# Moving a general-case branch into the attention loop, building the bias on ScalarE, and starting the gated products at the last scores

## The chip, the cores and the metric

The kernel runs on one core of one Trainium2 chip. The metric is the device time of one execution in microseconds (us), lower being better; the runs shown are whole executions, and one further execution was taken with the hardware profiler. Engines are named as in the profile: PE is TensorE (PEld its weight loads), DVE is VectorE, ACT is ScalarE, POOL is GpSimd, SP is SyncE, which issues most of the DMAs. A queue name ends in q (DVEq is VectorE's sequencer).

## What is computed

Three stages follow each other: attention with a window of local keys plus a few global ones, a gated feed-forward layer with RMS normalisation, and a routed layer with eight experts. Cut to what matters here:

```python
def _attn_ref(q, k, v, n_global, n_local):          # q, k, v: 2 x 8 heads x 768 x 64
    scores = scale * np.matmul(q, k.transpose(0, 1, 3, 2))
    rel = pos[:, None] - pos[None, :]
    keep = is_global | ((rel >= 0) & (rel < n_local))
    dist = np.where(is_global & ~is_local, n_local, np.abs(rel))
    scores = np.where(keep, scores - slopes[:, None, None] * dist, -1e9)
    a = np.exp(scores - scores.max(-1, keepdims=True))
    return np.matmul(a / (a.sum(-1, keepdims=True) + 1e-9), v)

def _moe_ref(x, w_gate, w_val, w_out, rms_g):       # x: 1536 x 512, w_gate, w_val: 512 x 1536
    xn = x / np.sqrt(np.mean(x * x, -1, keepdims=True) + 1e-6) * rms_g
    g = xn @ w_gate
    return (g * sigmoid(g) * (xn @ w_val)) @ w_out
```

`n_global` is 8 and `n_local` is 96. They are inputs, so the kernel reads them at run time: if the window is narrow enough it takes a fast path (a block of 64 queries sees at most 192 keys), else a general one. The routed layer behind it is not touched by the change.

## The kernel before

**Attention.** The sixteen heads are taken in eight pairs (`pr`), each pair's 768 queries in three groups (`g`) of 256: 24 items. `attention` is a generator of 28 steps `t`, a software pipeline of five stages: step `t` computes the scores of item `t` (`qk`, line 240), divides item `t-1` by its denominators (`zadd` L267, `zrec` L271, `norm` L278), transposes item `t-2` on TensorE (`trans`, L286) and copies it out of PSUM (`evac`, L295 and L297), multiplies item `t-3` with V (`pv`, L313), and hands item `t-4` to the normalisation (`out`). Between these, VectorE adds bias to the scores and takes their minimum in one custom operation (`ttr`, L251), and ScalarE takes the exponentials (`exp`, L262). Every engine executes in the order in which the code issues; nothing reorders it. Steps 24 to 27, without new scores, are the drain.

**Bias.** `consts` (L59 to L77) makes `s.nl` and `s.ng` from the integers, then the flag of the fast path, which every engine loads into a register (L77). Behind it stands `tc.If(flag == 0)` around `general_attention` (L985 in the rows). Then `bias_tiles` builds `keep` and `miss` (L106 to L109) and, with four VectorE operations for each of four pairs of heads (L112), the bias tiles: the first pair's before step 0, the others after steps 0, 1 and 2.

**Normalisation.** `Rms.take` (L414 to L416) splits each output into `xh` and `xl` and squares it on ScalarE (`sq`, a tile for each pair). `add` (L422) sums squares on GpSimd after pairs 1 and 2 of each batch, leaving two tiles. `stats` (L444) sums them over partitions with matmuls against a 128 by 128 tile of ones, two times six for a batch, after step 17 for the first batch and after steps 26 and 27 for the second. `root` (L448 to L472) computes an inverse square root on VectorE and six diagonal tiles, three of them on ScalarE; `spread` (L478, L481) turns these into rows by matmuls and copies them out on ScalarE.

**Weights and gated products.** The 64-bit weights come in units. `unpack` takes a unit apart in five parts: an absolute value on ScalarE (L489), a comparison on VectorE (L491), two bit operations on VectorE (L496, L498), and a last one (L501) with a cast on ScalarE (L503) and a subtraction on GpSimd (L504). Four units are wanted for the first products. From step 13 on, one part follows each step (`next(unit)`). `gemm1` (L538) is a gated product, 24 matmuls over 512 or 256 columns; `gate1` (L549 to L556) evaluates the gate of the product before it. The first three products are issued behind steps 25, 26 and 27, the fourth behind the root; then the spreading, then the loop over `order`, whose first product is `(0, 1, 256, 512)`.

Of the kernel before, what the change touches and what calls it, by code (L numbers as in the profile page):

```python
# [43 lines left out]
def consts(s, ints):  # L44
# [23 lines left out]
    s.ng, s.nl = s.gl[:, 0:1], s.gl[:, 1:2]  # L68
    a = c.tile([128, 3], F32, name="fasta")
# [24 lines left out]
def bias_tiles(s):  # L94

    nc = s.nc
    s.kinds = [0, 64, 192, 384]
    N = 576  # L100
    s.bias = s.apool.tile([128, 4, N], F32, name="bias", bufs=1)
    rel, key = s.rel[:, 0:N], s.rel[:, N:2 * N]
    keep, miss, slopes = s.keep, s.miss, s.slopes
    nc.gpsimd.tensor_copy(slopes, s.rel[:, 2 * N:])
    spans = [(0, 64, 0), (64, 192, 4), (192, 384, 0), (384, 576, 4)]
# [12 lines left out]
def general_attention(s):  # L118

    nc, tc = s.nc, s.tc  # L120
    with tc.tile_pool(name="ga", bufs=1) as p, tc.tile_pool(name="gap", bufs=1, space=PSUM) as ps:
        slopes = p.tile([128, 8, 2], F32, name="gslopes")
        for j in range(16):
            nc.gpsimd.memset(slopes[:, j // 2, j % 2:j % 2 + 1], -(2.0 ** -(j % 8 + 1)))
        with tc.For_i(0, 8, 1) as pr:
            slope = p.tile([128, 2], F32, name="gslope")
            nc.vector.tensor_copy(slope, slopes[:, ds(pr, 1), :].rearrange("p a b -> p (a b)"))
            for hh in range(2):
                r = slice(64 * hh, 64 * hh + 64)
                q = p.tile([64, 768], F32, name="gq")  # L130
                nc.sync.dma_start(q.rearrange("p (a n) -> p a n", a=1),
                                  s.qx.rearrange("a p n -> p a n")[r, ds(pr, 1), :])
                k = p.tile([64, 928], F32, name="gk")
                nc.sync.dma_start(k.rearrange("p (a n) -> p a n", a=1),
                                  s.kx.rearrange("a p n -> p a n")[r, ds(pr, 1), :])
                v = p.tile([128, 11, 64], F32, name="gv")
                nc.sync.dma_start(v.rearrange("p (a b) d -> p a b d", a=1),
                                  s.vx.rearrange("a p h b d -> p a h b d")[:, ds(pr, 1), hh])
                xo = p.tile([64, 768], F32, name="gxo")
                rel0 = p.tile([128, 768], F32, name="grel0")  # L140
                nc.gpsimd.iota(rel0, pattern=[[-1, 768]], base=0, channel_multiplier=1,
                               allow_small_or_imprecise_dtypes=True)
                key0 = p.tile([128, 768], F32, name="gkey0")
                nc.gpsimd.iota(key0, pattern=[[1, 768]], base=0, channel_multiplier=0,
                               allow_small_or_imprecise_dtypes=True)
                with tc.For_i(0, 6, 1) as i:
                    qi = p.tile([64, 128], F32, name="gqi")
                    nc.vector.tensor_scalar(qi.rearrange("p (a c) -> p a c", a=1),
                                            q.rearrange("p (i c) -> p i c", c=128)[:, ds(i, 1), :],
                                            0.125, None, ALU.mult)  # L150
                    rel = p.tile([128, 768], F32, name="grel")
                    nc.vector.tensor_copy(rel, rel0)
                    key = p.tile([128, 768], F32, name="gkey")
                    nc.vector.tensor_copy(key, key0)
                    loc = p.tile([128, 768], F32, name="gloc")
                    dist, keep = distance(s, rel, key, loc)
                    sc = ps.tile([128, 6, 128], F32, name="gsc")
                    for j in range(6):
                        nc.tensor.matmul(sc[:, j, :], lhsT=qi, rhs=k[:, 160 * j:160 * j + 128],
                                         start=True, stop=True)  # L160
                    t = p.tile([128, 768], F32, name="gt")
                    nc.vector.scalar_tensor_tensor(
                        out=t, in0=dist, scalar=slope[:, hh:hh + 1], in1=sc.rearrange("p a b -> p (a b)"),
                        op0=ALU.mult, op1=ALU.add)
                    nc.vector.tensor_tensor(t, t, keep, ALU.mult)
                    nc.vector.tensor_scalar(keep, keep, 1.0, -NEG, ALU.subtract, ALU.mult)
                    nc.vector.tensor_tensor(t, t, keep, ALU.add)
                    m = p.tile([128, 1], F32, name="gm")
                    nc.vector.tensor_reduce(m, t, AX.X, ALU.max)
                    nc.vector.tensor_scalar(t, t, m, None, ALU.subtract)  # L170
                    z = p.tile([128, 1], F32, name="gz")
                    nc.scalar.activation(t, t, AF.Exp, accum_out=z)
                    nc.vector.tensor_scalar(z, z, 1e-9, None, ALU.add)
                    nc.vector.reciprocal(z, z)
                    nc.vector.tensor_scalar(t, t, z, None, ALU.mult)
                    pt = ps.tile([128, 6, 128], F32, name="gpt")
                    for j in range(6):
                        nc.tensor.transpose(pt[:, j, :], t[:, 128 * j:128 * j + 128], s.ident)
                    pts = loc.rearrange("p (a b) -> p a b", a=6)
                    nc.vector.tensor_copy(pts, pt)  # L180
                    po = ps.tile([64, 128], F32, name="gpo")
                    for j in range(6):
                        nc.tensor.matmul(po, lhsT=v[:, 2 * j, :], rhs=pts[:, j, :],
                                         start=j == 0, stop=j == 5)
                    nc.vector.tensor_copy(xo.rearrange("p (i c) -> p i c", c=128)[:, ds(i, 1), :],
                                          po.rearrange("p (a c) -> p a c", a=1))
                    nc.vector.tensor_scalar(rel0, rel0, 128.0, None, ALU.add)
# [754 lines left out]
def attn_moe_kernel(ctx, tc, qx, kx, vx, rel, ints, wgv, w_out, rms_g, w9, w9t, w1, w2, out):  # L942
# [96 lines left out]
    for t in att:  # L1039
# [5 lines left out]
        if t >= 13:  # L1045
            next(unit, None)
# [384 lines left out]
```

## Time and profile before

| | us |
|---|---|
| median of three runs | 554.47 (553.97 to 555.34) |
| the profiled execution | 554.08, span 552.3 |
| first minimum of the scores starts | 10.12 |
| last item's denominators (step 24) | 90.63 |
| first gated product starts | 99.14 |
| statistics of the second batch done | 118.10 |
| product `(0, 1, 256, 512)` starts | 123.28 |

The span is the time from the first to the last instruction in the profile. The rows name an instruction by its line, engine, operation and tiles; a float32 matmul of the code leaves two records, one for each pass. A number in square brackets is the idle time of the engine just before the row, with what ended it.

### The profile page before, as it was taken

How to read it: one execution, taken by the hardware profiler on the slowest of the kernel's cores; microseconds unless marked ns; L12 is line 12 of the kernel's file. 1: busy time of each engine (PE TensorE's matmuls, PEld its weight loads, DVE VectorE, ACT ScalarE, POOL GpSimd, SP SyncE). 2: the span in 40 equal slices, each digit the busy share in tenths (PEclk: the TensorE clock that was granted, in tenths of full speed). 3: DMA queues.
4: the chain of work that ended last, by engine and by line, in shares of the span. 5: the costliest groups of instructions: out<-in, count | busy, mean ns of one | idle time of the engine just before them, and what ended most of it. 6: DMA issues, size and time to landing. Idle time of an engine off the chain costs nothing. (4 is left out here: it accounts for less than half of the span.)

```text
span 552.3 us, 9096 instructions
## 1 busy us (share of the span) xinstructions
PE 524.2 (95%) x3132; PEld 425.8 (77%) x3132; DVE 404.8 (73%) x1026; ACT 277.5 (50%) x631; POOL 140.8 (25%) x140
## 2 busy tenths in 40 slices
PE   3899886999999999999999999999999999999994
PEld 2676665878888888888888888878789787888883
DVE  5899999567888688868884358456443599999971
ACT  2799896324332233333333255244231587988850
POOL 2446545001222212212220200000000512666001
PEclk9999998999999999999999999999999999999998
DMA  8653511112323323323313512116171599999300
GB/s 301 210 211 139 173 36 39 33 46 77 105 88 113 113 79 114 114 79 113 115 38 130 214 39 78 39 52 215 39 293 57 202 393 395 398 399 396 131 15 16
DMA packets 28997, 80.62 MB, mean 146 GB/s; under 512 B 3512, under 2 KB 3768, under 8 KB 28945
## 3 DMA queue, kind: packets, MB, share of 16 engines
q1 hardware_dynamic: 24400, 68.61, 35.0%
q0 software_dynamic: 2672, 8.22, 3.9%
q10 hardware_dynamic: 1872, 3.15, 1.6%
q8 instruction: 26, 0.43, 0.3%
q14 instruction: 27, 0.21, 0.1%
HBM read 72.28 MB, written 8.65 MB: 147 GB/s over the span
## 5 line engine op out<-in xcount | busy, mean ns | idle before, releaser
L538 PE MATMUL ps<-xh,wh 128*128 128x512 f32 (+1 forms) x304 | 115.4, 380 | 0.1
L538 PE MATMUL ps<-xh,wl 128*128 128x512 f32 (+1 forms) x304 | 115.0, 378 | 0.5 <-POOL wl L504 0.5
L538 PE MATMUL ps<-xl,wh 128*128 128x512 f32 (+1 forms) x304 | 114.9, 378 | 0.0
L854 DVE TENSOR_TENSOR ewl<-eraw,ewh 128x1024 fp32r<-128x1024 f32 x72 | 83.5, 1220 | 6.2 <-ACT ewh L845 5.9
L845 ACT CAST ewh<-eraw 128x1024 fp32r<-128x1024 f32 x72 | 71.3, 1055 | 6.2 <-DVE ewl L854 4.2
L538 PEld LDWEIGHTS ps<-xh,wl 128*128 128x128 f32 x304 | 57.2, 188 | 11.6 <-POOL wl L504 0.9
L491 DVE SCALAR_TENSOR_TENSOR wraw<-f64t,wraw 128x512 f32<-128x512 f32 x36 | 44.7, 1241 | 28.8 <-ACT f64t L489 28.8
L538 PEld LDWEIGHTS ps<-xh,wh 128*128 128x128 f32 x304 | 57.2, 188 | 11.0 <-issue 0.7
L538 PEld LDWEIGHTS ps<-xl,wh 128*128 128x128 f32 x304 | 57.2, 188 | 10.6
L604 PE MATMUL px<-woh,hh 128*128 128x512 f32 (+1 forms) x156 | 61.8, 396 | 0.0
L604 PE MATMUL px<-woh,hl 128*128 128x512 f32 (+1 forms) x156 | 58.7, 376 | 0.0
L604 PE MATMUL px<-wol,hh 128*128 128x512 f32 (+1 forms) x156 | 58.2, 373 | 0.0
L504 POOL TENSOR_TENSOR wl<-f64t,wh 128x512 fp32r<-128x512 f32 x24 | 31.0, 1293 | 101.3 <-ACT wh L503 55.7
L503 ACT CAST wh<-f64t 128x512 fp32r<-128x512 f32 x24 | 14.9, 622 | 71.4 <-DVE f64t L501 68.1
L262 ACT ACTIVATE es<-es,m 128x192 f32<-128x192 f32 (+1 forms) x96 | 41.4, 434 | 11.5 <-DVE m L251 10.3
L278 POOL TENSOR_SCALAR es<-es,z 128x192 f32<-128x192 f32 x46 | 36.0, 791 | 36.2 <-ACT pts L297 11.7
L286 PE MATMUL pt<-ident,es 128*128 128x128 f32 x176 | 30.5, 305 | 10.1 <-DVE pts L295 6.6
L286 PEld LDWEIGHTS pt<-ident,es 128*128 128x128 f32 x176 | 20.7, 152 | 21.6 <-DVE pts L295 10.0
L568 DVE TENSOR_TENSOR hl<-h,hh 128x256 fp32r<-128x256 f32 x72 | 25.4, 422 | 15.8 <-ACT hh L567 15.8
L604 PEld LDWEIGHTS px<-woh,hl 128*128 128x128 f32 x156 | 29.3, 188 | 5.8
L604 PEld LDWEIGHTS px<-woh,hh 128*128 128x128 f32 x156 | 29.4, 188 | 4.9
L604 PEld LDWEIGHTS px<-wol,hh 128*128 128x128 f32 x156 | 29.5, 189 | 4.0
(195 smaller groups left out, 979.7 us busy)
## 6 DMA issues: line engine op xcount, KB each, us to landing
eraw<-in_w_dram SPq DMA_DIRECT2D x64, 512.0 KB, 11.2
wraw<-in_wgv_dram SPq DMA_DIRECT2D x24, 512.0 KB, 3.8
wraw<-in_w_out_dram SPq DMA_DIRECT2D x12, 512.0 KB, 3.5
vp<-in_vx_dram SPq DMA_DIRECT2D x8, 704.0 KB, 4.0
eraw<-in_w_dram POOLq DMA_DIRECT2D x8, 512.0 KB, 13.6
kd<-in_kx_dram SPq DMA_DIRECT2D x7, 464.0 KB
xm<-x SPq DMA_DIRECT2D x12, 256.0 KB
out_dram<-x ACTq DMA_DIRECT2D x12, 256.0 KB, 2.8
```

Source lines behind the costliest of these rows:

```text
L262: nc.scalar.activation(e[:, r, x, e0:e0 + n], e[:, r, x, e0:e0 + n], AF.Exp, bias=m[:, j:j + 1], scale=-1.0, accum_out=z[:, j:j + 1])
L278: eng.tensor_scalar(e[:, r, x, e0:e0 + n], e[:, r, x, e0:e0 + n], z[:, j:j + 1], None, ALU.mult)
L286: nc.tensor.transpose(pt[:, kt, x, :], e[:, r, x, 128 * kt:128 * kt + 128], s.ident)
L491: nc.vector.scalar_tensor_tensor(out=a.bitcast(F32), in0=t, scalar=F64_LEAST, in1=a.bitcast(F32), op0=ALU.is_ge, op1=ALU.mult)
L503: nc.scalar.copy(hi, t)
L504: eng.tensor_tensor(lo, t, f(hi), ALU.subtract)
L538: nc.tensor.matmul(p, lhsT=w[:, k, :], rhs=x[c][:, k, a:b], start=n == 0, stop=n == 11)
L568: nc.vector.tensor_tensor(hl[:, i, :], src, f(hh[:, i, :]), ALU.subtract)
L604: nc.tensor.matmul(p, lhsT=h[:, k, :], rhs=w[k][:, c:c + N], start=n == 0, stop=n == 35)
L845: eng.copy(wh, raw)
L854: eng.tensor_tensor(wl, raw, f(wh), ALU.subtract)
```

## The change

1. `general_attention` moves from the front of the program into the branch that already stood in the middle of the attention, which now comes after step 15 instead of 16. It is rewritten to use tiles that are there at that point. On the given inputs it is not executed. The flag is computed and loaded in a new function `windowed`, called behind the first piece of the bias.
2. The bias is scaled from one tile `dist` by a slope: `dist` takes three VectorE operations over 576 columns; of the eight scaled pieces seven are ScalarE copies with a scale, one is VectorE's.
3. `add` is called after pair 1 of each batch only, and `stats` works on three tiles of squares, against one column of ones.
4. Parts of units follow the steps from step 5 on, the first four gated products stand behind steps 24 to 27, and `(0, 1, 256, 512)` stands between root and spreading, with `Silu` as the gate of the product before it.

The core of the diff (the body of `general_attention` is left out):

```diff
@@ bias_tiles
-    s.kinds = [0, 64, 192, 384]
+    s.kinds = [0, 256, 64, 384]
...
-    nc.vector.tensor_scalar(keep, rel, s.nl, None, ALU.is_lt)
-    nc.vector.scalar_tensor_tensor(out=keep, in0=key, scalar=s.ng, in1=keep, op0=ALU.is_lt, op1=ALU.max)
-    nc.vector.tensor_scalar(miss, keep, 1.0, -8.0 * NEG, ALU.subtract, ALU.mult)
-    nc.vector.tensor_scalar(rel, rel, s.nl, None, ALU.min)
+    nc.vector.tensor_scalar(dist, rel, s.nl, -256.0 * NEG, ALU.is_ge, ALU.mult)
+    nc.vector.scalar_tensor_tensor(out=dist, in0=key, scalar=s.ng, in1=dist, op0=ALU.is_ge, op1=ALU.mult)
+    nc.vector.scalar_tensor_tensor(out=dist, in0=rel, scalar=s.nl, in1=dist, op0=ALU.min, op1=ALU.add)
     for hp in range(4):
-        for a, b, z in spans:
-            nc.vector.scalar_tensor_tensor(out=s.bias[:, hp, a:b], in0=rel[:, a:b],
-                                           scalar=slopes[:, z + hp:z + hp + 1],
-                                           in1=miss[:, a:b], op0=ALU.mult, op1=ALU.add)
+        nc.scalar.activation(s.bias[:, hp, 0:256], dist[:, 0:256], AF.Copy, scale=slopes[:, hp:hp + 1])
+        if hp:
+            nc.scalar.activation(s.bias[:, hp, 256:N], dist[:, 256:N], AF.Copy, scale=slopes[:, 4 + hp:5 + hp])
+        else:
+            nc.vector.tensor_scalar(s.bias[:, hp, 256:N], dist[:, 256:N], slopes[:, 4:5], None, ALU.mult)
         yield
@@ attention
-            if pr % 4 in (1, 2) and t == 3 * pr + 8:
+            if pr % 4 == 1 and t == 3 * pr + 8:
                 rms[pr // 4].add()
@@ Rms.stats
-                nc.tensor.matmul(self.ss[:, j:j + 128], lhsT=sq[:, 128 * j:128 * j + 128], rhs=s.ones,
+                nc.tensor.matmul(self.ss[:, j:j + 1], lhsT=sq[:, 128 * j:128 * j + 128], rhs=s.ones[:, 0:1],
@@ attn_moe_kernel
-    flag = consts(s, ints)
+    consts(s, ints)
     bias = bias_tiles(s)
-    with tc.If(flag == 0):
-        general_attention(s)
...
     next(bias)
+    flag = windowed(s)
...
-        if t >= 13:
+        if t >= 5:
             next(unit, None)
-        if t == 16:
+        if t == 15:
             with tc.If(flag == 0):
+                general_attention(s)
                 rms[0].general(s.xg)
...
-        if t in (25, 26, 27):
+        if t in (24, 25, 26, 27):
             gemm1s()
...
     run(rms[1].root())
-    while done[0] < 4:
-        gemm1s()
+    step1((0, 1, 256, 512))
     for z in range(3):
         rms[1].spread(z, s.bank([128, 256], "rb"))
...
-    for x in order:
+    for x in order[1:]:
```

How the order on the engines changes is shown at three places. The first is VectorE at the end of step 6, before (es is the tile of probabilities, z the denominators, xl the low part of an output):

```order
L295 COPY pts<-pt 128x512
L416 SCALAR_TENSOR_TENSOR xl_337<-po,rg,xh_336 128x256
L267 TENSOR_SCALAR z<-z 128x4
L271 RECIPROCAL z<-z 128x4
L278 TENSOR_SCALAR es_366<-es_366,z 128x64
```

And after:

```order
L296 COPY pts<-pt 128x512
L417 SCALAR_TENSOR_TENSOR xl_133<-po,rg,xh_132 128x256
L492 SCALAR_TENSOR_TENSOR wraw<-f64t,wraw 128x512
L268 TENSOR_SCALAR z<-z 128x4
L272 RECIPROCAL z<-z 128x4
L279 TENSOR_SCALAR es_174<-es_174,z 128x64
```

A part of an unpacking (wraw is the raw unit) now stands between two steps there, ahead of the next denominators; before, the first such part on VectorE stood behind step 14.

The second place is TensorE behind the last scores, in steps 23 to 25, before (pt are transposes, po products with V, ps the gated product's two sums):

```order
L286 MATMUL pt<-ident,es_366 128x128 x6
L313 MATMUL po<-pts,vp 64x128 x8
L286 MATMUL pt<-ident,es_367 128x128 x8
L313 MATMUL po<-pts,vp 64x128 x6
L286 MATMUL pt<-ident,es_368 128x128 x8
L313 MATMUL po<-pts,vp 64x128 x8
L538 MATMUL ps_1755<-xh_330,wh_1057 128x512
```

And after:

```order
L287 MATMUL pt<-ident,es_174 128x128 x6
L314 MATMUL po<-pts,vp 64x128 x8
L287 MATMUL pt<-ident,es_175 128x128 x8
L314 MATMUL po<-pts,vp 64x128 x6
L539 MATMUL ps_1720<-xh_126,wh_433 128x512
```

The first gated product has moved ahead of the last eight transposes and the product with V behind them; the other products have moved ahead by one step each, and `(0, 1, 256, 512)` stands where the fourth one stood, under the root.

The third place is ScalarE at the root of the second batch, before (rd are the diagonal tiles, sg the gates, rs the copied rows, f64t a unit's first part):

```order
L472 ACTIVATE rd<-ident,r_1949 128x128 x3
L551 ACTIVATE sg<-h_364 128x512
L481 COPY rs_338<-rb 128x256
L481 COPY rs_323<-rb 128x256 x2
L551 ACT_TABLE_LOAD
L551 ACTIVATE sg<-h_365 128x256
```

And after:

```order
L473 ACTIVATE rd<-ident,r_1967 128x128 x3
L552 ACT_TABLE_LOAD
L552 ACTIVATE sg<-h_173 128x256
L482 COPY rs_134<-rb 128x256
L482 COPY rs_119<-rb 128x256 x2
L490 ACTIVATE f64t<-wraw 128x512
```

The table load and the gate that needs it have moved from behind the three copies to ahead of them.

## Rows read from the trace of the kernel before

**Rows 1.** The page, busy time of each engine: us, share of span, instructions.

```profile
PE 524.2 (95%) x3132; PEld 425.8 (77%) x3132; DVE 404.8 (73%) x1026; ACT 277.5 (50%) x631; POOL 140.8 (25%) x140
```

**Rows 2.** Table of windows: stretch, its length, busy time by engine, TensorE's clock.

```profile
30.00:40.00 10.00, 9.91 (x142) 7.21 (x138) 9.58 (x48) 9.97 (x40) 5.40 (x8) 1.00 0.60 215
...
90.00:92.00 2.00, 1.44 (x12) 1.06 (x13) 1.79 (x3) 2.00 (x8) 2.00 (x2) 1.00 0.01 2
92.00:94.00 2.00, 1.18 (x12) 0.78 (x8) 1.93 (x4) 1.52 (x5) 1.58 (x2) 0.50 0.04 8
...
96.00:98.00 2.00, 2.00 (x13) 1.67 (x14) 1.78 (x4) 0.43 (x1) 0.00 (x0) 0.50 0.00 0
...
126.00:140.00 14.00, 14.00 (x76) 12.12 (x75) 11.87 (x20) 4.57 (x10) 2.58 (x2) 1.00 0.24 75
```

**Rows 3.** The flag's load (ns), then the timeline of the start: start, length, instruction.

```profile
L77 PEldq TENSOR_LOAD <-fasti x1: 493/493/493, 5.4 to 5.4; - x1
...
5.21 0.15 DVE L76 CAST fasti<-fast 128x1 int32<-128x1 f32 x1
...
6.77 2.74 PE L240 MATMUL sc<-kd,qd 64*64 64x64 f32 x32 [6.77 <-DVEq L985]
7.29 0.82 DVE L107 SCALAR_TENSOR_TENSOR keep<-rel,gl,keep 128x576 f16<-128x576 f16 x1
...
10.12 0.22 DVE L251 CUSTOM_DVE_ANT_0 es<-sc,bias 128x64 f32<-128x64 f32 x1
```

**Rows 4.** Timeline of steps 0 and 1: a bias group, and ScalarE's first exponential.

```profile
11.03 1.21 DVE L112 SCALAR_TENSOR_TENSOR bias<-rel,slopes,miss 128x64 f32<-128x64 f16 x4
...
13.13 0.46 ACT L262 ACTIVATE es<-es,m 128x192 f32<-128x192 f32 x1 [1.04 <-DVE m L251]
```

**Rows 5.** Timeline of VectorE: the denominators of steps 6, 12, 13 and 24.

```profile
28.64 0.17 DVE L267 TENSOR_SCALAR z<-z 128x4 f32<-128x4 f32 x1 [0.21 <-ACT es L262]
...
46.13 0.98 DVE L267 TENSOR_SCALAR z<-z 128x4 f32<-128x4 f32 x1 [0.21 <-ACT es L262]
...
49.76 0.15 DVE L267 TENSOR_SCALAR z<-z 128x4 f32<-128x4 f32 x1
...
90.63 1.41 DVE L267 TENSOR_SCALAR z<-z 128x4 f32<-128x4 f32 x1 [0.21 <-ACT es L262]
```

**Rows 6.** Timeline: an addition of squares, two comparisons of a unit, the statistics' reader.

```profile
54.83 1.82 POOL L422 TENSOR_TENSOR sq<-sq 128x768 f32<-128x768 f32 x1
...
55.40 1.80 DVE L491 SCALAR_TENSOR_TENSOR wraw<-f64t,wraw 128x512 f32<-128x512 f32 x1
...
68.37 0.17 DVE L448 TENSOR_SCALAR rv<-po 128x6 f32<-128x6 f32 x1 [1.01 <-PE po L444]
...
76.01 0.69 DVE L491 SCALAR_TENSOR_TENSOR wraw<-f64t,wraw 128x512 f32<-128x512 f32 x1
```

**Rows 7.** Timeline of weight loads: statistics, product with V, logits.

```profile
65.38 2.75 PEld L444 LDWEIGHTS po<-ones,sq 128*128 128x128 f32 x24 [0.17 <-issue]
...
104.83 0.90 PEld L313 LDWEIGHTS po<-pts,vp 128*64 128x64 f32 x16 [0.35 <-issue]
...
315.79 1.09 PEld L589 LDWEIGHTS lg<-w9t,x2t 128*128 128x128 f32 x8
```

**Rows 8.** Timeline of the drain: TensorE's waits, the root's diagonals, the table load.

```profile
91.77 1.41 PE L313 MATMUL po<-pts,vp 128*64 128x128 f32 x12
...
95.51 1.97 PE L286 MATMUL pt<-ident,es 128*128 128x128 f32 x8 [2.33 <-DVE pts L295]
...
114.49 0.19 PEld L538 LDWEIGHTS ps<-xh,wl 128*128 128x128 f32 x1 [0.87 <-POOL wl L504]
...
120.58 0.99 ACT L472 ACTIVATE rd<-ident,r 128x128 f32<-128x128 f32 x3 [7.18 <-DVE r L464]
...
122.84 0.52 PEld L478 LDWEIGHTS rb<-rd,ones 128*128 128x128 f32 x4 [0.88 <-ACT rs L481]
...
123.98 1.28 ACT L551 ACT_TABLE_LOAD   x1
```

More of the change, by code (lines that the diff above doesn't have):

```diff
@@ L118, in general_attention @@
 def general_attention(s):
[L120 to L141, printed above, removed]
@@ new lines, in general_attention @@
+    nc, tc, p = s.nc, s.tc, s.apool
+    slopes = p.tile([128, 8, 2], F32, name="gslopes", bufs=1)
+    for j in range(16):
+        nc.gpsimd.memset(slopes[:, j // 2, j % 2:j % 2 + 1], -(2.0 ** -(j % 8 + 1)))
+    one, two = (s.h[c, 0].rearrange("p a b -> p (a b)") for c in range(2))
+    rel, key = one[:, 0:768], two[:, 0:768]
+    qi, xo = one[0:64, 768:896], one[0:64, 896:1024]
+    ks = [two[0:64, 768 + 128 * j:896 + 128 * j] for j in range(2)]
+    ks += [s.rs[2][0:64, 128 * j:128 * j + 128] for j in range(4)]
@@ L142, in general_attention @@
                                allow_small_or_imprecise_dtypes=True)
-                key0 = p.tile([128, 768], F32, name="gkey0")
-                nc.gpsimd.iota(key0, pattern=[[1, 768]], base=0, channel_multiplier=0,
+                nc.vector.tensor_scalar(rel, rel, first, None, ALU.add)
+                nc.gpsimd.iota(key, pattern=[[1, 768]], base=0, channel_multiplier=0,
                                allow_small_or_imprecise_dtypes=True)
[L146 to L161, printed above, removed]
-                    nc.vector.scalar_tensor_tensor(
[L163 to L187, printed above, removed]
@@ L188, in general_attention @@
-                nc.sync.dma_start(s.xg.rearrange("(a h p) n -> p a h n", h=2, p=64)[:, ds(pr, 1), hh, :],
-                                  xo.rearrange("p (a n) -> p a n", a=1))
+                dist, keep = distance(s, rel, key, loc)
+                for h in range(2):
+                    sc = s.ps_g.tile([128, 3, 128], F32, name="gsc", tag="ps0", bufs=2)
+                    for j in range(3):
+                        nc.tensor.matmul(sc[:, j, :], lhsT=qi, rhs=ks[3 * h + j], start=True, stop=True)
+                    c = slice(384 * h, 384 * h + 384)
+                    nc.vector.scalar_tensor_tensor(
+                        out=t[:, c], in0=dist[:, c], scalar=slope[:, hh:hh + 1],
+                        in1=sc.rearrange("p a b -> p (a b)"), op0=ALU.mult, op1=ALU.add)
@@ L192, in attention @@
+                for j in range(6):
+                    nc.tensor.matmul(po, lhsT=v[:, 2 * j, :], rhs=pts[:, j, :], start=j == 0, stop=j == 5)
+                nc.vector.tensor_copy(xo, po)
+                nc.sync.dma_start(
+                    s.xg.rearrange("(a h p) (i c) -> p a h i c", h=2, p=64, c=128)[:, ds(pr, 1), hh, ds(i, 1), :],
+                    xo.rearrange("p (a b c) -> p a b c", a=1, b=1))
+                nc.vector.tensor_scalar(first, first, 128.0, None, ALU.add)
 def attention(s, rms):
@@ L1386, in relative @@
     far = FAR16
-    parts = [(64, 0, 0), (128, 64, 0), (96, 96, far), (32, None, 0), (64, 0, far),
-             (32, 96, far), (32, None, 0), (128, 64, far)]
+    parts = [(64, 0, 0), (96, 96, far), (32, None, 0), (64, 0, far), (128, 64, 0), (32, 96, far), (32, None, 0), (128, 64, far)]
     row = (np.arange(128) % 64)[:, None]
```

50 lines of the change are left out of this document (43 added, 7 removed).

## The prediction

> **What bounds the kernel now.** I read the page's busy times first: TensorE is busy 95% of the span, VectorE 73% [rows 1]. That share is a mean over unlike stages, so the table of windows came next, where the reader should see three regimes. In the attention steps (30 to 40 us) ScalarE is busy 9.97 of 10 us and VectorE 9.58 [rows 2]: these two bound a step, and work added to either lengthens it. From 126 us on TensorE is busy 14.00 of 14.00 at full clock and waits for nothing [rows 2]; a delay made before that point therefore reaches the end, and so does a gain. In between lies the drain, 92 to 123 us, where TensorE has idle time and its granted clock reads 0.50, the lower level of 1.2 GHz [rows 2]. After the windows I read the timeline of the start [rows 3, 4], the starts of the denominator operation of each step, which give its pace [rows 5], the steps that hold unpacking parts [rows 6], and the drain [rows 8].
>
> The profiled execution took 554.08 us (span 552.3); the median of the three runs is 554.47, 0.39 more, less than the runs differ. I add to 554.08. A measurement of this kernel tells some 0.3% (1.7 us) from no change.
>
> **The start.** Today VectorE finishes the flag's cast at 5.21 + 0.15 = 5.36, the register load takes 0.49, and with the jump TensorE starts at 6.77; VectorE then builds the bias, and the first minimum starts at 10.12 [rows 3]. The jump goes. But in the new order the cast stands behind three passes over 576 columns and one over 320, and TensorE's first instruction is still the load of that flag. Two of the passes have the form of L107, 0.82 each [rows 3]; the other two read one wide tensor and are cheaper; I take 2.6 for the four, between 1.64 (those two alone) and 3.3 (all at 0.82). So: flag at 5.36 + 2.6 = 8.0, loaded at 8.5, then the first step's scores, which are 16 of the 32 records that took 2.74 [rows 3], say 1.25, and the first minimum at 9.7 instead of 10.12: **-0.4** (-1.3 to +0.4).
>
> **Bias by ScalarE.** VectorE loses a group of four operations of 1.21 in each of steps 0 to 2 [rows 4]. They ran while ScalarE did the exponentials, and the next step waits for those, so little comes back: **-0.1** (-0.5 to +0.2). ScalarE gets two scaled copies instead. A pass over 192 columns takes it 0.46, so 256 and 320 columns cost some 0.5 each; they stand behind the exponentials, where ScalarE idles 1.04 until the next minimum [rows 4]. That idle time is the cover; without it each step would cost 1.0 more.
>
> **Unpacking from step 5.** This is the largest term. A weight unit is unpacked in five parts, one a step, now from step 5 instead of 13: eight more parts inside the steps, and eight fewer in the drain, where they cost one wait of 0.87 [rows 8]. Steps 6 to 12, without parts, run at (46.13 - 28.64)/6 = 2.92 us; steps 13 to 24, with eleven parts, at (90.63 - 49.76)/11 = 3.72 [rows 5]. The excess is 8.8 us. Of it 1.0 is VectorE's wait for the statistics, and 1.1 is the operation L491 drawn out from 0.69 to 1.80 while GpSimd adds squares [rows 6]. 6.7 are left for eleven parts and the root; giving the root 0.8 to 2.5 leaves 0.38 to 0.54 a part, so eight cost 3.0 to 4.3. The operations alone say the like: the eight parts hold six on VectorE, up to 0.69 each, and three on ScalarE, both nearly full there. I take **+4.0** (2.4 to 5.2; the upper end because GpSimd's part of a unit, a subtraction over 512 columns, can hold VectorE up as its addition does in [rows 6]).
>
> **One addition of squares less.** The add after step 14 goes, so nothing draws an operation there out: **-1.1** (-1.1 to -0.5). The one after step 26 lay in the drain, beside other work.
>
> **Statistics.** With three tiles of squares instead of two, 12 matmuls become 18, of one column instead of 128; each leaves two records, so 24 become 36. VectorE waits for the last: 1.01 before 68.37 [rows 6], and all that follows in its queue, ScalarE too, waits with it. The 24 weight loads took 2.75, 0.111 apart; the logits, nine columns wide with the same 128 weight columns, took 1.09 for eight, 0.129 apart [rows 7]. So narrow moving data buys nothing, the weights set the pace, and 36 take 4.0 to 4.6: **+1.4** (+1.2 to +1.9; -0.75 if the weights didn't bind, by the third of the rivals). The Trainium skill (TensorE: Matmul & The Clock Gate, section Back-to-back issue gap) gives about 60 cycles for a matmul of up to 64 columns, 25 ns at full clock; by that alone 36 records would take 0.9 and this term would be -1.9. The logits' row disagrees, and the row decides.
>
> **The branch at step 15.** It takes the place of the one after step 16, and no row of the steps around that one ends a wait of VectorE on a jump: the wait before 68.37 is for TensorE [rows 6]. The body jumped over is far longer now. I take **+0.1** (0 to +0.9, the price of a bare jump under the rivals).
>
> **The drain.** Before, from the product with V at 91.77, TensorE waits 2.33 for VectorE's copies, and transposes (1.97 for eight) and product run at the lower clock, some 1.6 lost; later comes the 0.87 wait for GpSimd [rows 8]. The first gated product, put right behind the product at 91.77, needs none of that and hides it: -4.8. Against this: (a) the lower level falls on that product instead. TensorE is at 0.50 from 92 to 98 [rows 2], and the new product takes the place of the transposes and product that lost some 1.6 there, so I charge it the same: +1.6. (b) 12 more statistics records, +1.4. (c) ScalarE's table load of 1.28 came at 123.98, behind the three copies of the root [rows 8]; now it stands ahead of them, the third spreading waits for the first copy's bank, and TensorE's next product with it: the diagonals end at 120.58 + 0.99 = 121.57, and load, a short gate and a copy (some 0.4 each) behind them end at 123.65, where the third spreading started at 122.84 [rows 8]: +0.8. (The root itself stays under a gated product of the same length as before.) Together **-1.0** (-2.6 to +0.6).
>
> **Sum.** -0.4 - 0.1 + 4.0 - 1.1 + 1.4 + 0.1 - 1.0 = +2.9, so 557.0.
>
> **Rivals.** (1) TensorE stays at 2.4 GHz through the drain, because the new product closes the gap in time: term (a) goes, 555.4, no change that can be measured. For it: the clock was still full up to 92, with TensorE idle 0.56 of the last 2 us [rows 2]. Against: the product at 91.77 took 1.41 [rows 8] and lies in the low stretch already, before the new one would start. It decides if the new product's 24 matmuls keep one spacing throughout. (2) The steps are VectorE's budget from the start: the 3 x 1.21 taken from steps 0 to 2 come back whole and pay for the parts. 557.0 - 3.5 = 553.5, not slower; with the clock high too, 551.9. For it: VectorE's high share [rows 2]. Against: ScalarE's 1.04 of idle and the chain through the exponentials [rows 4]. It decides if the fifth denominator starts at least 1.7 earlier. (3) One-column matmuls are paced by columns: the cheapest weight row here, 64 columns wide, has 16 in 0.90, 0.056 apart [rows 7]; 36 of those take 2.0, which saves 2.1 against my sum at step 17 and as much in the drain: 552.8, faster. Against it stands the logits' row. (4) The jump stalls. At the start it took 6.77 - 5.36 - 0.49 = 0.9 beyond the load [rows 3]; if each engine pays that once at step 15, over the same long body, 557.8. The Trainium skill (Runtime: NRT & Kernel Launch, section Instruction fetch mechanics) says that a taken branch out of the fetched pages waits for a fetch; no row here separates that from the jump.
>
> **How the numbers follow.** Chances: forecast 0.45 (slower 0.37, same 0.06, faster 0.02); clock 0.20 (0.05, 0.13, 0.02); budget 0.15 (0, 0.07, 0.08); columns 0.08 (0, 0.03, 0.05); jump 0.12 (0.11, 0.01, 0). That is slower 0.53, same 0.30, faster 0.17. The terms' ends don't add, as they are independent: around 557.0 I allow 2.8 up, to 559.8. Downwards the range takes in the clock, the budget and most of the columns' case: 552.4. About 0.1 lies beyond each end.
>
> **What would show it.** First minimum at 9.7; fifth denominator no more than 0.6 earlier than now; steps 5 to 12 at 3.3 to 3.5 us; 36 statistics records in over 4 us; a gated product right behind the last scores' step, at half pace first; the table load between root and copies. Wrong would be above all: parts that vanish in the steps, or statistics in 2 us.

## The result and the profile after

The changed kernel takes 561.30 us (median; 560.95 to 561.98) where the kernel before takes 554.22: a ratio of 1.0126, with a 95% interval of 1.0105 to 1.0147. It is slower, as forecast, but by 7.1 us instead of 2.5, and outside the range, which ended at 559.8.

The span of the profiled execution grew from 552.3 to 559.6. From the page, busy time of each engine (us, share of the span, instructions), which answers to [rows 1]:

```profile
PE 529.8 (95%) x3156; PEld 432.2 (77%) x3156; DVE 397.6 (71%) x1010; ACT 280.1 (50%) x638; POOL 136.5 (24%) x138
```

The shares hardly move, so the loss has to be found by stage. The table below has one row for each stretch between the starts of two denominators (the operation of [rows 5], numbered by step), and a last one from step 24's to the first matmul that has both the spreading and the product `(0, 1, 256, 512)` behind it. It is worked out from the timelines of the two kernels; from that matmul on both do the same work at full pace.

| stretch | before | after | measured | predicted |
|---|---|---|---|---|
| start to step 5 | 25.29 | 25.60 | +0.31 | -0.5 |
| 5 to 13 | 24.47 | 27.83 | +3.36 | +4.0 |
| 13 to 15 (an addition less) | 7.36 | 6.79 | -0.57 | -1.1 |
| 15 to 17 (branch) | 6.83 | 8.81 | +1.98 | +0.1 |
| 17 to 18 (statistics) | 4.50 | 7.88 | +3.38 | +1.4 |
| 18 to 24 | 22.18 | 24.20 | +2.02 | 0 |
| 24 to that matmul | 35.64 | 32.46 | -3.18 | -1.0 |
| sum | 126.27 | 133.57 | +7.30 | +2.9 |

The rows that this rests on, first of before: the denominators of steps 5, 15, 17 and 18 (those of 13 and 24 are in [rows 5]) and the matmul that ends the table (start, length, instruction):

```profile
25.29 0.17 DVE L267 TENSOR_SCALAR z<-z 128x4 f32<-128x4 f32 x1
...
57.12 0.16 DVE L267 TENSOR_SCALAR z<-z 128x4 f32<-128x4 f32 x1
...
63.95 0.17 DVE L267 TENSOR_SCALAR z<-z 128x4 f32<-128x4 f32 x1
...
68.45 0.94 DVE L267 TENSOR_SCALAR z<-z 128x4 f32<-128x4 f32 x1
...
126.27 0.40 PE L538 MATMUL ps<-xh,wh 128*128 128x512 f32 x1
```

Then of after: the denominators of steps 5, 13, 15, 17, 18 and 24, with the statistics' reader between them, and the matmul at the end:

```profile
25.60 0.17 DVE L268 TENSOR_SCALAR z<-z 128x4 f32<-128x4 f32 x1
...
53.43 0.16 DVE L268 TENSOR_SCALAR z<-z 128x4 f32<-128x4 f32 x1
...
60.22 0.16 DVE L268 TENSOR_SCALAR z<-z 128x4 f32<-128x4 f32 x1
...
69.03 0.16 DVE L268 TENSOR_SCALAR z<-z 128x4 f32<-128x4 f32 x1
...
76.83 0.17 DVE L449 TENSOR_SCALAR rv<-po 128x6 f32<-128x6 f32 x1 [4.44 <-PE po L445]
76.91 0.16 DVE L268 TENSOR_SCALAR z<-z 128x4 f32<-128x4 f32 x1
...
101.11 0.16 DVE L268 TENSOR_SCALAR z<-z 128x4 f32<-128x4 f32 x1
...
133.57 0.48 PE L539 MATMUL ps<-xh,wh 128*128 128x512 f32 x1
```

Two rows stand out. VectorE waits 4.44 us for the statistics, 1.01 before [rows 6]. And between steps 15 and 17 something new is in the timeline of TensorE: the next scores wait for VectorE's end of the branch of line 1047 (PE row), which lies behind VectorE's last work of that step (first row):

```profile
63.72 0.47 DVE L417 SCALAR_TENSOR_TENSOR xl<-po,rg,xh 128x256 fp32r<-128x256 f32 x1
...
64.39 1.68 PE L241 MATMUL sc<-kd,qd 64*64 64x192 f32 x16 [2.41 <-DVEq L1047]
```

The table of windows (stretch, length, busy time by engine, granted clock in the third column from the right, as [rows 2]) shows what before has nowhere in the steps, TensorE at the lower level while it is busy all the time:

```profile
72.00:76.00 4.00, 4.00 (x31) 4.00 (x31) 0.39 (x2) 0.92 (x4) 0.00 (x0) 0.81 0.55 180
76.00:80.00 4.00, 4.00 (x30) 3.11 (x32) 2.76 (x22) 2.10 (x9) 1.53 (x2) 0.50 0.01 2
102.00:120.00 18.00, 18.00 (x122) 15.39 (x120) 9.22 (x19) 6.20 (x12) 1.29 (x1) 1.00 0.09 31
120.00:128.00 8.00, 7.70 (x54) 7.65 (x55) 0.34 (x2) 0.00 (x0) 0.00 (x0) 0.79 0.01 3
```

The 36 statistics records lie from 71.59 to 76.79 and, in the drain, at 119.03 and 126.07. In the timeline of TensorE the first are

```profile
71.59 5.20 PE L445 MATMUL po<-ones,sq 128*128 128x1 f32 x36
```

Behind these the clock is 0.50, behind those of the drain 0.79; before, both places read 1.00. (It also reads 0.57 from 64 to 68 us, behind TensorE's wait at the branch.)

The drain itself is better than forecast. The first gated product starts right behind the last product with V but two, at full pace (0.34 behind its first matmul, then 0.22 to 0.24 from matmul to matmul to its last), and the transposes behind it wait for nothing. What the profile shows at its end is the table load between the root's diagonals and the copies, and TensorE's wait for the first copy, 1.34 in its row, which was 0.69 before (0.88 on the weight load in [rows 8]):

```profile
130.07 0.99 ACT L473 ACTIVATE rd<-ident,r 128x128 f32<-128x128 f32 x3 [12.21 <-DVE r L465]
131.08 1.28 ACT L552 ACT_TABLE_LOAD   x1
...
133.10 0.71 PE L479 MATMUL rb<-rd,ones 128*128 128x128 f32 x4 [1.34 <-ACT rs L482]
```

### The profile page after: what moved, and what is told of

The parts are those of the page before. It is cut to its first block, busy times and chain, and to the rows that moved or that the text cites. A ratio compares the mean times of both kernels' runs of the same rounds, so it can differ in the third digit from the quotient of the medians.

```text
span 559.6 us, 9122 instructions
## 1 busy us (share of the span) xinstructions
PE 529.8 (95%) x3156; PEld 432.2 (77%) x3156; DVE 397.6 (71%) x1010; ACT 280.1 (50%) x638; POOL 136.5 (24%) x138
## 5 line engine op out<-in xcount | busy, mean ns | idle before, releaser
L241 PE MATMUL sc<-kd,qd 64*64 64x192 f32 (+2 forms) x384 | 24.4, 375 | 11.4 <-DVE fasti L81 9.0
```

The source lines that it names most:

```text
L241: nc.tensor.matmul(sc[x][o, r, 0:n], lhsT=qs[pr][d, i:i + 64], rhs=ks[pr][d, k0:k0 + n], start=True, stop=True)
```

## The experiments

Times are medians beside runs of the kernel before on the same chip; ratios are to those. The stretches in the readings are those of the table above.

**Statistics of 128 columns.** The changed kernel with

```diff
-nc.tensor.matmul(self.ss[:, j:j + 1], lhsT=..., rhs=s.ones[:, 0:1],
+nc.tensor.matmul(self.ss[:, j:j + 128], lhsT=..., rhs=s.ones,
```

> The changed kernel with one edit: each statistics matmul is 128 columns wide again (36 records, three tiles of squares, all else as changed). In the changed kernel the 36 one-column records at step 17 took 5.20 us, and the granted clock read 0.81 while they ran and 0.50 in the 4 us behind them; in the drain it read 0.79 at the second group of records. Theory A (one-column matmuls bring TensorE's clock down): with wide matmuls the clock stays at 1.00 behind the statistics, the 36 records take 4.0 to 4.4 us at 0.111 to 0.12 apart, the next steps lose nothing, and the time falls by 2 to 3.5 us to 558 to 559.5. Rival B (the clock falls because TensorE waited 2.41 us at the branch before, and narrow or wide plays no part): the clock reads the same as in the changed kernel, 36 records take about 5, and the time stays at 561 (within 0.8). Rival C of my prediction (narrow moving data are cheaper): the time rises by 1 to 2.

Measured: 558.27, ratio 1.0051 (1.0032 to 1.0069), 3.0 less than the changed kernel. Its statistics row and its windows, of the same stretches as above:

```profile
72.62 4.29 PE L445 MATMUL po<-ones,sq 128*128 128x128 f32 x36
...
72.00:76.00 4.00, 4.00 (x42) 3.83 (x39) 1.38 (x7) 1.96 (x9) 0.00 (x0) 1.00 0.55 182
76.00:80.00 4.00, 4.00 (x61) 3.19 (x59) 3.06 (x23) 2.59 (x11) 1.64 (x2) 1.00 0.01 2
...
120.00:128.00 8.00, 7.70 (x66) 7.54 (x65) 2.55 (x15) 0.56 (x2) 0.00 (x0) 1.00 0.01 2
```

36 records take 4.29 instead of 5.20, and the clock behind them reads 1.00 in both places. Steps 18 to 24 take 22.85 (24.20), the drain 31.07 (32.46). Theory A holds. The wait at the branch is still there, and with it a stretch at 0.50 ahead of the statistics (64 to 68 us), so the two causes are separate. The stretch from 17 to 18 is not shorter, 8.32 (7.88): VectorE's wait in it falls from 4.44 to 3.57, but TensorE comes to the records later, as its clock reads 0.70 from 68 to 72 us in this execution, where the changed kernel's reads 1.00. So in the time the narrow form's price shows behind this stretch and not in it.

**Two tiles of squares.** The changed kernel with GpSimd's second addition in each half back (`pr % 4 in (1, 2)`), so 24 one-column records.

> The changed kernel with one edit undone: GpSimd adds the squares twice in each half again, so the statistics read two tiles (24 one-column records instead of 36). My prediction's terms: one addition less gains 1.1 at step 14, 12 records more cost 1.4 at step 17 and 1.4 in the drain, so this should give 561.3 + 1.1 - 2.8 = 559.6. Theory A (VectorE's wait for the statistics grew from 1.01 to 4.44 us, because each record at the lower clock takes 0.144 and because TensorE comes late to them): 24 records at 0.144 take 3.5, and the wait falls to about 2.7; time 559 to 560. Rival (the wait is set by where TensorE stands when it comes to them, not by their number): the wait stays above 4 and the time is 561 to 562.5, as the added addition costs and nothing is gained.

Measured: 557.48, ratio 1.0051 (1.0036 to 1.0065). The row of the statistics:

```profile
72.02 2.84 PE L445 MATMUL po<-ones,sq 128*128 128x1 f32 x24
```

The addition costs what was forecast for it: 13 to 15 takes 7.90 instead of 6.79, +1.1. Against that stand 17 to 18 with 6.12 instead of 7.88, 18 to 24 with 23.61 instead of 24.20, and the drain with 29.62 instead of 32.46; there the clock stays at 1.00 behind 16 and 8 records. So 12 records are worth more than their own 1.4 each time, and the gain, 3.8, is larger than theory A's 1.7, as is the fall of VectorE's wait (to 1.94, where theory A had 2.7). The rival falls.

**The branch with a short body.**

```diff
 with tc.If(flag == 0):
-    general_attention(s)
     rms[0].general(s.xg)
```

> The changed kernel with the general attention left out of the branch at step 15 (the body is only the general path of the statistics; the kernel then has no general attention at all, which its inputs here do not need). In the changed kernel TensorE waited 2.41 us for VectorE's join of that branch, and step 16 and 17 each ran about 1.0 us longer than before. Theory A (the body uses the score banks, so behind the join TensorE's next scores wait until VectorE has drained all work of step 15): the wait goes, steps 15 to 17 gain 1.5 to 2.5 us, time 558.5 to 560. Rival B (jump over a long body, which needs a fetch): the wait goes too, which the next kernel tells apart. Rival C (the wait is the price of any branch at this place, as before at step 16): the wait stays, time 561.3 within 0.6.

Measured: 558.63, ratio 1.0067 (1.0054 to 1.0080), 2.7 less. No wait for line 1047 is left in TensorE's timeline; 15 to 17 takes 7.60 (8.81) and 17 to 18 6.75 (7.88), since TensorE no longer comes late to the statistics.

**One score bank used in the short body.** A matmul into a tile of tag `ps0` and VectorE's copy of it are put into the body.

> The kernel before it in this list (short body, no general attention), with one matmul into a score bank and one copy of it by VectorE put into the body, which is jumped over all the same. Theory A (dependence of the score bank on the join): TensorE waits for VectorE's join again, 1.5 to 2.6 us, and the time goes back to within 0.6 of 561.3. Rival B (fetch behind a long jump): the body is short, so there is no such wait, and the time is that of the short body, 558.5 to 560.

Measured: 559.13, ratio 1.0075 (1.0062 to 1.0088). No wait. Taken alone this spoke for rival B. But there are two buffers of each tag, and the next scores take the other one, so the edit had not put the dependence where the long body puts it. The next two take the theories apart.

**A long body without banks.** The long body stays, with its loops and loads, but TensorE's work and the copies out of PSUM in it are left out.

> The changed kernel, whose branch at step 15 keeps a long body with its three nested loops, but the body uses no PSUM bank and TensorE does nothing in it (its matmuls, transposes and the copies out of PSUM are left out, so the general attention it would compute is not right; it is jumped over here). The short body measured 558.6 us against 561.3, and one matmul in one of the two score banks put into it did not bring the wait of 2.41 us back. Theory A (score banks: all four of them are used in the long body, so that behind the join TensorE's next scores wait for VectorE): no wait of TensorE for VectorE's join, steps 16 to 18 as with the short body, 558 to 559.5. Rival B (length: the jump ends in code that has to be fetched): TensorE waits 1.5 us or more at the join again, 560.5 to 562.

Measured: 558.35, ratio 1.0083 (1.0061 to 1.0106). 15 to 17 takes 7.60, as with the short body.

**A short body with all four score banks.**

```diff
 rms[0].general(s.xg)
+for h in range(2):
+    for x in range(2):
+        gb = s.ps_g.tile([128, 3, 128], F32, name="gsc", tag=f"ps{x}", bufs=2)
+        nc.tensor.matmul(gb[:, 0, :], lhsT=s.ident, rhs=s.ones, ...)
+        nc.vector.tensor_copy(gx[:, 0:128], gb[:, 0, :])
```

> The changed kernel with the general attention left out of the branch at step 15, but with four matmuls and four copies by VectorE in the short body that use all four score banks, two of each tag, as the long body does (jumped over all the same). Theory A (score banks): TensorE's next scores wait for VectorE's join again, 1.5 to 3 us; steps 16 to 18 as in the changed kernel; time 560.5 to 562. Rival B (length of the jump): no wait, 558 to 559.5.

Measured: 561.68, ratio 1.0138 (1.0112 to 1.0163). The scores of the same step in the two kernels, the long body without banks first (it has no wait; its line numbers are ten lower), then the short one with them:

```profile
62.11 0.88 PE L231 MATMUL sc<-kd,qd 64*64 64x192 f32 x16
...
64.37 1.56 PE L241 MATMUL sc<-kd,qd 64*64 64x192 f32 x16 [2.32 <-DVEq L1047]
```

Theory A is shown: the banks make the wait, the length of what is jumped over doesn't. The Trainium skill (Runtime: NRT & Kernel Launch, section Instruction fetch mechanics) says that a taken branch out of the fetched pages waits for a fetch; at this branch no row shows such a wait.

**Parts from step 13 again.** The changed kernel with `t >= 13` for `t >= 5`.

> The changed kernel with the unpacking parts from step 13 again, as before; the first gated product then has its two units ready at step 22, and the parts that are left stand in the drain. My prediction priced the eight early parts at 4.0 us in the steps, and what they save in the drain at 0.9. Forecast by that: step 13 starts 3 to 4 us earlier (denominator at 49.6 to 50.5 instead of 53.43), the drain loses 0.9 to 2, time 558 to 560. Rival (the parts fill time that TensorE or VectorE waits anyway further on, at the statistics and the join): the gain up to step 13 is lost by step 24 and the time is 561 to 563.

Measured: 559.87, ratio 1.0106 (1.0079 to 1.0133). The time is in the forecast's range and the rival falls, but both amounts of the forecast were too small: 5 to 13 takes 24.14 (27.83), step 24 comes at 91.31 (101.11), 9.8 earlier, and the drain takes 38.41 (32.46). In the drain the third product now waits for its weights: 1.28 for `wh`, 0.62 for `wl`, and once more 0.63 and 0.62, and the clock falls to 0.73 behind that and the one-column records. So of the 9.8 that late parts gain, the drain takes 6.0 back. The wait at the branch is still there, but it is 1.37 instead of 2.41, and 15 to 17 takes 7.54 (8.81): part of the branch's price hangs on the early parts. (The profiled execution, 557.73, lies 2.1 below the median, so the median's gain is the smaller, 1.4.)

**The new drain in the kernel before.** Gated products at steps 24 to 27 and the one of (0, 1, 256 to 512) ahead of the spreading; nothing else.

> The kernel before with one thing of the change alone: the four first gated products stand at steps 24 to 27, and the one of (0, 1, 256 to 512) ahead of the spreading. My prediction gave the new drain -4.8 for the waits it covers, +1.6 for the clock in the first product, +1.4 for 12 more statistics records (not in this kernel) and +0.8 for the table load. In the changed kernel that product ran at full clock, so +1.6 should be gone. Theory A: -4.8 + 0.8 = -4.0, 550 to 551.5 (before: 554.5). Rival (the units of the second pair are not unpacked in time, so TensorE waits in the drain where it didn't): -1 to +1, 553.5 to 555.5.

Measured: 554.63, ratio 1.0010 (0.9990 to 1.0030): nothing, so the rival holds. Its third product and the window around it:

```profile
104.57 0.50 PE L538 MATMUL ps<-xh,wh 128*128 128x512 f32 x1 [1.29 <-ACT wh L503]
105.93 0.56 PE L538 MATMUL ps<-xh,wl 128*128 128x512 f32 x1 [0.63 <-POOL wl L504]
...
104.00:112.00 8.00, 6.80 (x21) 4.88 (x22) 5.93 (x9) 2.66 (x6) 2.56 (x2) 0.79 0.42 133
```

The drain takes 35.26 (35.64 before; the profiled execution, 552.52, lies 2.1 below its median). Its gain needs the units in time; the early parts of the change are what pays for that.

**One-column statistics in the kernel before.** The first edit of this section, the other way round.

> The kernel before with one thing of the change alone: the statistics matmuls are one column wide instead of 128 (two tiles of squares, 24 records, the branch where it was). Theory A (one-column matmuls bring the granted clock down, with no wait at a join ahead of them): the 24 records take 2.7 to 2.9 us as before, but the clock, 1.00 before, reads 0.5 to 0.9 in the 8 us behind them at step 17, and time rises by 0.5 to 2, to 555 to 556.5. Rival (it was the wait at the join or the number of records): clock 1.00 there and time 554.5 within 0.6. Third (narrow is cheaper): records in 2 us and the time lower.

Measured: 554.33, ratio 0.9987 (0.9973 to 1.0001). The window behind the statistics, of this kernel and then of before:

```profile
68.00:72.00 4.00, 4.00 (x33) 3.15 (x32) 3.05 (x21) 2.39 (x8) 2.92 (x3) 0.57 0.73 257
...
68.00:72.00 4.00, 3.71 (x55) 2.61 (x54) 3.63 (x22) 2.39 (x11) 2.93 (x3) 1.00 0.62 206
```

The clock falls here too, with no wait at a branch ahead of it. But the time doesn't follow: with 24 records and TensorE on time, step 17 to 18 takes 4.55 instead of 4.50. That the narrow form costs only where TensorE comes late is how I read the two experiments together; no run tests it by itself.

**Bias by ScalarE in the kernel before.** The new `bias_tiles` alone, behind the jump of the start.

> The kernel before with one thing of the change alone: the bias tiles are made by ScalarE's scaled copies from one distance tile (first one partly by VectorE); the jump at the start stays. My prediction gave -0.1 (-0.5 to +0.2) for it, with the cover of ScalarE's idle time. Forecast: the fifth denominator 0 to 0.6 earlier, time 553.9 to 554.6. Rival (ScalarE's copies lie on the chain of the first steps): each of steps 1 to 3 is up to 1.0 longer, 555 to 557. Rival (VectorE is what steps 0 to 3 wait for): 2 to 3.5 us earlier, 551 to 552.5.

Measured: 555.64, ratio 1.0021 (1.0012 to 1.0030), about +1.0 us. The first denominator starts at 13.51 (12.15 before; 12.11 to 12.79 over the four kernels with the old start and the old bias). The timeline of the start shows why:

```profile
9.67 1.28 ACT L109 ACT_TABLE_LOAD   x1 [9.67 <-DVE dist L107]
...
11.51 0.23 DVE L250 CUSTOM_DVE_ANT_0 es<-sc,bias 128x64 f32<-128x64 f32 x1 [1.42 <-ACT bias L109]
```

ScalarE's table load now stands behind the distance tile and ahead of its first copy, and the first minimum waits 1.42 for that copy; the other kernel with this bias and the old start (three parts in each of steps 24 to 27, below) has the same wait. Before, the load ran from 6.47 on, and the first minimum waited for nothing. In the changed kernel the load starts at 7.32, and the first minimum, at 10.54, waits for the scores, so it is covered. The fifth denominator, 25.93, tells nothing: over the four kernels it varies from 24.43 to 25.92. And the profiled execution, 552.89, lies 2.75 below its median, so the 1.0 itself can't be followed to its end here.

**The three faults mended.** The changed kernel with wide statistics, two tiles of squares, and the general attention's PSUM tiles in the transposes' tag:

```diff
-s.ps_g.tile([128, 3, 128], F32, name="gsc", tag="ps0", bufs=2)
+s.ps_n.tile([128, 3, 128], F32, name="gsc", tag="rb", bufs=2)
```

(and the same for `gpt`).

> The changed kernel with what the experiments pointed at mended at once: the general attention in the branch uses the bank of the transposes instead of the four score banks, the statistics matmuls are 128 columns wide and read two tiles of squares. Single edits gave -2.7 (no wait at the join), -3.0 (wide) and -3.8 (two tiles) against 561.3. Theory A: the three share one loss (the lag of TensorE and its clock at step 17), so they do not add: 555 to 556.5, what is left over the 554.4 of before being the early parts less the drain. Rival: they add, 551.5 to 553. Second rival: transposes wait for the join in the scores' place, 557 to 558.5.

Measured: 555.14, ratio 1.0008 (1.0000 to 1.0017). Single gains of 3.0, 3.8 and 2.7 make 6.2 together, as theory A's range has it, but not for theory A's reason. By the stretches of the profiles, from 15 to 24, where TensorE's lag is, they nearly add: 0.9, 2.9 and 1.8 singly, 5.3 together. In the drain they don't: 1.4, 2.8 and nothing singly, 2.7 together, as wide records and fewer records mend the same loss of the clock. The rest, 1.8, lies ahead of step 5 (0.3, 0.8 and 0.7 singly, nothing together), where these kernels don't differ: it is the spread of single executions. The wait is now one of the transposes, in TensorE's timeline:

```profile
65.83 0.85 PE L287 MATMUL pt<-ident,es 128*128 128x128 f32 x6 [2.48 <-DVEq L1047]
```

It costs nothing: 15 to 17 takes 7.58 (7.60 with the short body), since the next scores are already made.

**Three parts in each of steps 24 to 27.** Kernel before with the new drain, the new bias, Sigmoid, and more parts at the drain's beginning.

> A version meant to beat both: the kernel before (parts from step 13, wide statistics of two tiles, its branches where they were) with the bias by ScalarE, the new order of the gated products in the drain, three unpacking parts instead of one in each of steps 24 to 27, and the gate before the spreading by Sigmoid, so that no table load stands ahead of the root's copies. The new drain alone measured 554.6, with 1.29 + 0.62 us of waits for units not yet unpacked ahead of its third product, the clock at 0.79 over 8 us there, and 1.33 ahead of the third spreading. Theory A (parts in the drain's first steps are covered by the first two products): these waits go, -2 to -4, 550.5 to 552.5. Rival (the parts hold up VectorE's copies for the last transposes, so the second product comes later by what the third gains): 553.5 to 555.

Measured: 554.05, ratio 0.9996 (0.9982 to 1.0010). The third product still waits, 1.55 and 0.62: VectorE works its queue in order, and the parts of step 25 stand behind a copy of that step that waits 4.22 for TensorE. The time is the rival's; in it is also what the new bias costs behind the old start. Sigmoid did its part: no wait ahead of the third spreading is left.

**Nine parts in step 24, in both kernels.** They stand ahead of that copy now, where VectorE has time.

```diff
-next(unit, None)
+for _ in range(9 if t == 24 else 1):
+    next(unit, None)
```

In the kernel before, with the new drain and Sigmoid:

> The kernel before with its old start, old bias, old branches and wide statistics of two tiles; new are the order of the gated products in the drain, nine unpacking parts in step 24, ahead of the first gated product, where VectorE waits 4.22 us for TensorE in the next step, and Sigmoid instead of Silu ahead of the root's copies. Theory A (early parts eat the drain's gain): the third product waits for no unit (1.55 + 0.62 before, in the version with three parts in each of steps 24 to 27) and the clock stays up, 549.5 to 552. Rival B (the nine parts hold up the next step's copy and with it the last transposes): 553.5 to 555.

And in the changed kernel with the three faults mended, parts from step 13 and Sigmoid:

> The changed kernel with the three faults mended (general attention of the branch in the transposes' bank, wide statistics, two tiles), and with late parts instead of early ones: from step 13, nine of them in step 24, and Sigmoid ahead of the root's copies. It differs from the kernel beside it by the new start with ScalarE's bias, the jump that is gone from the start and the branch at step 15. Theory A (early parts eat the drain's gain, the start is worth nothing either way): within 1 us of the kernel beside it, 549.5 to 552. Rival C (the new start costs what the bias alone did): 1 to 2 us slower than it.

Measured: 550.32, ratio 0.9933 (0.9909 to 0.9956), and 550.25, ratio 0.9932 (0.9913 to 0.9951). Both beat both kernels, by 3.6 us the kernel before. The spreading and the first product behind it, in the kernel before so edited, come without a wait:

```profile
118.57 1.85 PE L478 MATMUL rb<-rd,ones 128*128 128x128 f32 x12
...
120.18 0.48 PE L538 MATMUL ps<-xh,wh 128*128 128x512 f32 x1
```

That is 29.93 from step 24 on, 5.7 less than before (this kernel has the old bias, so it is not the place of the parts alone that tells it from the one before). The medians are equal, and the first kernel's runs lie from 548.44 to 551.65, so the new start, the jump that goes and the branch at step 15 are together worth nothing that these runs can tell, once the branch leaves the score banks alone. Theory A holds and rival C falls.

## Why the prediction was right in sign and wrong in size

The direction came out as forecast, but hardly for its main reason, that the early parts cost more than the drain returns. With the three faults mended, the kernel still has the early parts and the new drain, and it takes 1.0008 of the time before (1.0000 to 1.0017), some 0.4 us. The rest of the 7.1 us, over 6, is the branch, which I had at +0.1, and the statistics, which I had too small. So the right sign is in good part luck. Step by step:

- **Start (-0.4 predicted).** The cast ended at 8.29, near the 8.0 assumed; but TensorE began at 9.03, not 8.5, and its first scores took 1.5, not 1.25, so the first minimum stood at 10.54. A gain turned into a loss of 0.4. The fifth denominator varies by more than that, from 24.84 to 25.68 over kernels that share this start, with the clock between 10 and 30 us (0.83 to 1.00).
- **Bias (-0.1).** From the first to the fifth denominator 13.05 instead of 13.14: near, within what kernels of one start differ there (12.32 to 13.14 with the old), and rival 2 (3.5 to be gained) fell. I had left out ScalarE's table load of 1.28 ahead of the first copy. The new start covers it; behind the old one the same bias cost 1.0.
- **Parts (+4.0).** By step 13 right (+3.36 against before; 3.97 between the kernels with early and late parts, both mended). But those two differ by another 2.68 between steps 13 and 24 (43.51 against 40.83), where I had counted nothing, since eleven parts lie there either way. By the code the eleven are not alike: nine operations of VectorE against eight, 0.7. In the profiles VectorE is busy 39.91 us of that stretch against 38.59, 1.3 more; why the rest is lost was not settled. What failed in this term is its price, an average over parts, and that it was counted in eight steps only.
- **One addition less (-1.1).** Right: its return cost 1.11 (6.79 to 7.90 from 13 to 15). The table has only -0.57 there, as the early parts add 0.54 (7.90 with them, 7.36 without, both with the addition).
- **Statistics (+1.4).** The weights do pace the records (24 one-column records in 2.74, 0.114 apart), as the logits' row said, so rival 3 fell. The 60 cycles of the Trainium skill (TensorE: Matmul & The Clock Gate, section Back-to-back issue gap), which I had set against that row, are the gap of a matmul by itself; for a stream the same section lets weight load and matmul set the spacing together, and the trace agrees. This term failed by its size: 5.20 for 36 where I had 4.0 to 4.6, at the lower clock; VectorE's wait grew by 3.4, and 17 to 18 by 3.38 where I had 1.4. Of that, 12 records fewer gave back 1.76 and the wait at the branch removed 1.13, each by itself; wide records gave back nothing there, but 1.35 in 18 to 24 and 1.39 in the drain. I had weighed one column only as a possible gain.
- **Branch (+0.1).** The step that failed outright. I looked for a wait of VectorE at the old branch, whose body holds no work of TensorE and touches no score bank, and asked what a longer jump costs. The wait was TensorE's, 2.41, and its price a dependence: what the body would write. Removing it gave 2.7 where I had 0.1. Rival 4 (557.8) did give the branch a price, but too small a one, and by the wrong mechanism.
- **Drain (-1.0).** Better than forecast, -3.18. Term (a), +1.6 for the lower clock in the first product, did not come: 1.00 from 102 to 120 us, one spacing throughout, which is what rival 1 asked for. Terms (b) and (c) came, (b) larger: 12 records fewer gave 2.84 in the drain, and the table load stood where it was expected.

For the kernel with the three faults mended my terms give 557.0 + 1.1 for the second addition - 2.8 for 24 records fewer = 555.3, and it measured 555.14. So what took the time out of the range is the branch's wait and the 36 narrow records with the clock behind them; that the rest agrees is partly luck, since the parts were priced too low by 2.7 and the drain's gain too low as well.

## What to carry to other kernels

A branch that is never taken can still cost what its body touches: here an engine that needed a buffer of the body next waited, behind the branch, for the other engine's end of it. Give the body buffers that are not needed next, or whose next user has time to wait, as the transposes had. Work moved out of a stage must be put where its engine waits in its queue's order, not merely earlier: the same parts that cost 6.7 us in the steps found their place ahead of a copy that waits for the first product, which, with Sigmoid, made the mended kernel 4.2 us faster (ratios 1.0008 and 0.9932).

## What the runs showed of the hardware

TensorE's clock fell behind one-column matmuls although TensorE had been busy 4.00 of 4.00 us: 0.50 behind 36 records, 0.57 behind 24 in the kernel before, 1.00 behind wide ones in the same places. In the drain, 16 and then 8 one-column records left it at 1.00. The Trainium skill (TensorE: Matmul & The Clock Gate, section HAM oscillation — how this bites in real kernels) tells of a clock lost in gaps, where TensorE waits for data; here no gap was there. What it costs is seen in the product behind the drain's records, one matmul of 256 columns with one column in the statistics and the like with 128:

```profile
123.15 0.41 PE L539 MATMUL ps<-xh,wh 128*128 128x256 f32 x1
...
121.90 0.28 PE L539 MATMUL ps<-xh,wh 128*128 128x256 f32 x1
```

Of the first product's matmuls 17 in a row stand 0.21 to 0.22 apart; behind its first matmul the second's stand 0.11 to 0.12 apart to the end.
